# An attention and MLP kernel on one Trainium2 core: part of the splitting of the activations moves from VectorE to GpSimd, GpSimd's work is counted per step, and an order written out by hand begins at unit 2 instead of unit 8

## The chip, the cores and the metric

The kernel runs on one core of one Trainium2 chip. A core has five engines, each with its own instruction queue that is worked off in order: TensorE (PE in the profile, with PEld for its weight loads), VectorE (DVE), ScalarE (ACT), GpSimd (POOL) and SyncE (SP, which here issues every transfer). They meet only in semaphores. The metric is the device time of one execution in microseconds (us).

## The reference

Attention with a learned bias on the distance of positions, for 4 batches, 8 heads, 576 positions and 64 numbers a head, and behind it an MLP with a squared ReLU on the joined heads:

```python
scores = scale * np.matmul(q, k.transpose(0, 1, 3, 2))
x = (psi_rel / psi_i)[..., None]
bias = np.maximum(x @ w1 + b1, 0.0) @ w2
scores = scores + bias.transpose(2, 0, 1)[None, :, :, :]
attn = np.exp(scores - np.max(scores, axis=-1, keepdims=True))
attn = attn / (np.sum(attn, axis=-1, keepdims=True) + 1e-09)
attn_out = np.matmul(attn, v)
...
h = x @ w_in                # x: 2304 x 512, w_in: 512 x 2048
r = np.maximum(h, 0.0)
return (r * r) @ w_out      # w_out: 2048 x 512
```

## The kernel before

**Units.** Attention is cut into 80 units (b, hp, ic): a batch, a pair of heads and a block of 128 queries (ic 0 to 3) or the last 64 (ic 4, the tail, both heads side by side). Units 0 to 39 are batches 0 and 1: first the eight tails (units 0 to 7), then block by block. Units 40 to 79 are batches 2 and 3, five units for each pair of heads, so that units 44, 49, 54, ... 79 are tails. A unit goes through these steps: score products on TensorE (`score_products`, L425) into the one PSUM buffer `sp`; VectorE adds the bias and finds the row minimum (`reduce`, L438, one instruction for each head, only one for a tail), which frees `sp` for the next unit's products; ScalarE takes the exponential (L445); for a tail GpSimd copies 64 columns of the result (L447); TensorE transposes it in two pieces, `pp` (L529) and `pa` (L521), a tail's `pa` reading the copy; ScalarE copies these to `pt` (L851, L1122); TensorE multiplies by v into `px` (L547). When a head pair is done, VectorE inverts its sums (L459, L460), GpSimd makes three low-precision parts of them (L464 to L469), TensorE spreads these (`rp`, `ra`), and VectorE multiplies (L496).

**The bias** is made in the first units: VectorE compares a mask (`bias_mask`, L373), TensorE sums over 32 hidden numbers (`bb`, L383), ScalarE and VectorE scale the two halves (L388, L391) and GpSimd adds them (L399). `mask_upto` and `bias_upto` say how far masks and sums have gone; in the first eight steps each unit but the first two also carries a piece of the remaining mask thresholds (L328 to L332).

**Order.** `step(s)` emits the work of unit s with that of units s - 2 (transposes) and s - 3 (values). For the first `AB * HP` = 8 steps a scheduler orders the instructions of the engines; from step 8 on `manual_schedule` keeps the order in which the code emits them. From unit 40 on the code keeps a list of jobs, each a row of stages (engine, cost in us, function). `fill` takes a stage when its time has come and `room` of its engine is not used up. `room` is refilled at every step for DVE (1.65, or 2.5 at a tail) and ACT; POOL has no entry, so its stages are always taken at once.

**Splitting the activations.** The MLP's first matrix product is done by Strassen's seven products, in two 16-bit parts for each operand. For batch n, `x_scaled` queues products m = 3, 1, 7, 4, 6, 2, 5. Products 2 and 5 take a block of the activations, the other five a sum or difference of two blocks:

```python
stages.append(("POOL", 1.3, lambda m=m: sums_x(0, (m,))))      # L779: the sum, 128 x 512
stages.append(("ACT", 0.71, lambda m=m: high_x(0, (m,))))      # L785: high part, scaled by xsig
stages.append(("DVE", 0.74, lambda m=m: low_x(0, (m,))))       # L792: sum * xsig - high part
```

Batches 0 and 1 are split in this way between units 50 and 79; batches 2, 3 and the tails later, inside the MLP (`split_at`), by the same three functions. Other jobs of the same stretch prepare weights: `lead` (L195 on ACT, L197 to L201 on DVE), `sums_in` (L720 to L722) and the first `high_in` (L734) on POOL, `high_in` (L732) on ACT, `low_in` (L738) on DVE, `rest_out` (L707) on POOL.

**The MLP** begins when attention ends: `products` (`ha`, `hb`, L1191), `sums` (L1205 to L1210), `squares`, `parts_g` and `down` (`y`, L1283).

Of the kernel before, what the change touches and what calls it, by code (L numbers as in the profile page):

```python
# [17 lines left out]
ALU = mybir.AluOpType  # L18
# [4 lines left out]
HP = H // 2  # L23
# [4 lines left out]
AB = 2  # L28
# [49 lines left out]
def attention_then_relu2_mlp(ctx: ExitStack, tc: tile.TileContext, q, k, v, cols, w_in, w_out, psi, xmat, dist, out):  # L78
    nc = tc.nc
    PE, DVE, ACT, POOL, SP = nc.tensor, nc.vector, nc.scalar, nc.gpsimd, nc.sync  # L80
# [64 lines left out]
    NA = len(units)  # L145
# [352 lines left out]
    def scale_x(b, hp, rows_t):  # L498
        times_rows(b, hp, *spread_rows(rows_t))
# [163 lines left out]
    wdst, xsig, alpha_t = {}, {}, {}  # L663
# [72 lines left out]
    def low_in(n, which=(0, 1)):  # L736
# [5 lines left out]
    width = [256] * B + [128]  # L742
    RIGHT = {
        2: ((0, 0), None, None), 5: ((1, 1), None, None), 3: ((0, 1), ALU.subtract, (1, 1)), 4: ((1, 0), ALU.subtract, (0, 0)),
        1: ((0, 0), ALU.add, (1, 1)), 6: ((0, 0), ALU.add, (0, 1)), 7: ((1, 0), ALU.add, (1, 1)),
    }
    ORDER = (2, 3, 4, 5, 1, 6, 7)
    xs_t = {}
# [15 lines left out]
    split_to = [{m: operand(t[:, 512 * (m - 1):512 * m]) for m in range(1, 8)} for t in xs_at]  # L764
# [7 lines left out]
    def sum_of(n, m):  # L772
        return sum_at.get((n, m), sum_at.get(m))

    def sums_x(n, ms):
        for m in ms:
            for cs, op, a, b in halves(n, m):
                if op:
                    POOL.tensor_tensor(out=sum_of(n, m)[:, :, cs], in0=a, in1=b, op=op)  # L779

    def high_x(n, ms):
        for m in ms:
            hi = split_to[n % 2][m][0]
            for cs, op, a, b in halves(n, m):
                ACT.activation(out=hi[:, :, cs], in_=sum_of(n, m)[:, :, cs] if op else a, func=AF.Identity, scale=xsig[n])  # L785

    def low_x(n, ms):
        w = width[n]
        for m in ms:
            hi, lo = split_to[n % 2][m]  # L790
            for cs, op, a, b in halves(n, m):
                DVE.scalar_tensor_tensor(out=lo[:, :, cs], in0=sum_of(n, m)[:, :, cs] if op else a, scalar=xsig[n], in1=hi[:, :, cs], op0=ALU.mult, op1=ALU.subtract)  # L792
            xs_t[n, m] = (hi[:, :, :w], lo[:, :, :w])

    def store_x(n):
        xs_dram[n] = dram.tile([128, 7 * 512], F32, name=f"xs{n}")
        SP.dma_start(out=xs_dram[n], in_=xs_at[n % 2])
# [40 lines left out]
    def step(s, plain=True):  # L838
        loads(s)
        if plain:  # L840
            scores(s)
        else:
            negm, sps = score_products(s, False)
            exps = [reduce(s, n, negm, sp) for n, sp in enumerate(sps)]
        if s and rest:
            tc.keep_in_program_order(rest.pop(0)())
        n, r = divmod(s, AB * HP)

        def turned():
            for dst, src in transposes((s - TL,)):  # L850
                ACT.copy(dst, src)  # L851

        if not plain:
            rows_made(s - TL)
            turned()
            inverted(s - 1)
            if s >= AB * HP * TAIL:
                scan_first(s)
        if n < TAIL:
            if r == 7 and n + 2 < NIC:  # L860
                tc.keep_in_program_order(scale_xc(chunks[n + 2]))
            if plain:
                bias_upto(NJB * n + BO[r])
                if s == AB * HP - 1:
                    mask_upto(done + MB)
            else:

                def then():
                    mask_upto(done + MB + 1)
                    if exps:  # L870
                        exps.pop(0)()

                sum_upto(NJB * n + BO[r], then)
            if r == 1 and n + 2 < NIC:
                load_xc(chunks[n + 2])
        if plain:
            if s >= TL:
                turned()
        else:
            for fn in exps:  # L880
                fn()
        u = s - TL - 1
        if u >= 0:
            for piece in values((u,)):
                keep_values(*piece)
            if u in norm_of:
                b, hp, ic = units[u]
                scale_x(b, hp, norm_of.pop(u))
# [11 lines left out]
        if u in norm_of:  # L900
            norm_of[u] = norm_copy(norm_rows(norm_of[u]))

    for s in range(AB * HP):
        step(s)
    with tc.manual_schedule(engines={PE.engine, DVE.engine, ACT.engine}):
        for s in range(AB * HP, NA):
            step(s, False)

    scan_stack.close()
# [10 lines left out]
    room = {}  # L920
# [95 lines left out]
    def x_scaled(n, ps_col):  # L1016
        scale_of(n, ps_col)
        if n == 0:
            place_x = raw_tile("w2")
            free = [place_x[:, 512 * k:512 * k + 512] for k in range(2)]  # L1020
            for k, ms in enumerate(((3, 1, 7), (4, 6), (2, 5))):
                stages = []
                for m in ms:
                    if RIGHT[m][1]:
                        sum_at[m] = free[k].rearrange("p (c t) -> p c t", c=2)
                        stages.append(("POOL", 1.3, lambda m=m: sums_x(0, (m,))))
                    stages.append(("ACT", 0.71, lambda m=m: high_x(0, (m,))))
                    stages.append(("DVE", 0.74, lambda m=m: low_x(0, (m,))))
                jobs.insert(len(norms), [max(now[0], first[groups[AB * HP + AB]] + 1), stages])
        else:  # L1030
            free = [a.rearrange("p (c t) -> p c t", c=2) for a in (take(1, 4480, 512), take(0, 9856, 512))]
            for k, ms in enumerate(((3, 1, 7), (4, 6), (2, 5))):
                stages = []
                for m in ms:
                    if RIGHT[m][1]:
                        sum_at[n, m] = free[k]
                        stages.append(("POOL", 1.3, lambda m=m: sums_x(n, (m,))))
                    stages.append(("ACT", 0.71, lambda m=m: high_x(n, (m,))))
                    stages.append(("DVE", 0.74, lambda m=m: low_x(n, (m,))))
                job(dest_at[-1] + 1, *stages)  # L1040

    dest_at = [50] + [60] * 6 + [70]
# [49 lines left out]
    sum_at = {}  # L1092
    with tc.manual_schedule():
        job(NA + 1, *(("DVE", 0.68, lambda k=k: scan(k)) for k in range(SCANS, NF)))
        x_job(NA + 4, 0)
        x_job(NA + 7, 1)
        for u in range(NA - TL - 1, NA):
            norm_job(u)
        for s in range(NA, NU + TL + 3):
            now[0] = s  # L1100
            full = s < NU and units[s][2] < TAIL
            room["DVE"] = min(room.get("DVE", 0), 0.3) + (1.65 if full else 2.5)
            room["ACT"] = min(room.get("ACT", 0) + (0.55 if full else 1.9), 0.6 if full else 1.5)
            loads(s)
            if s == NA:
                for tag, name in zip("dbac", ("pa", "pp", "pp", "px")):
                    held[tag] = bank(name, tag)
                for m, tag in enumerate(raws[:NF - SCANS]):
                    fetch_in(ins[SCANS + m], tag)
            if s < NU:  # L1110
                negm, sps = score_products(s, False)
            fill(s, 3)
            px_now[0] = None
            us = [u for u in ((s - 3, s - 2) if s % 2 else (s - 2, s - 1)) if u < NU]
            pieces = []
            sms = [lambda n=n: softmax(s, n, negm, sps[n]) for n in range(len(sps))] if s < NU else []
            if s % 2 == 0:
                if s == NA and NA - 3 in pt_t:
                    for piece in values((NA - 3,), "c"):
                        keep_values(*piece)  # L1120
                for m, c in enumerate(transposes(us, iter("bacb" if s == NA else "abca")) if us else ()):
                    ACT.copy(*c)  # L1122
            else:
                pieces = values(us, "d") if us else []
            fill(s, 0)
            for fn in sms:
                fn()
            if s < NU and ends(s):
                norm_job(s)
            kept = 0  # L1130
            if any(j[0] <= s and j[1][0][0] == "LAST" for j in jobs):
                kept = max(room["DVE"] - 0.6, 0)
                room["DVE"] -= kept
            fill(s, 1)
            fill(s, 2)
            for piece in pieces:
                keep_values(*piece)
            if kept:
                room["DVE"] += kept
                fill(s, 1)  # L1140
# [31 lines left out]
    sum_at = {3: xT[0][:, 0:2, 128:384], 4: xT[0][:, 2:4, 128:384], 1: take(0, 9856, 512).rearrange("p (c t) -> p c t", c=2)}  # L1172
# [121 lines left out]
    with tc.manual_schedule():  # L1294
# [3 lines left out]
        for i in range(NI + 1):  # L1298
# [4 lines left out]
            n, P = items[min(i, NI - 1)]  # L1303
# [102 lines left out]
```

## Time and profile before

| what | us |
|---|---|
| median of 3 runs (714.94 to 715.3) | 715.07 |
| time of the profiled execution | 715.1 |
| its span, first to last instruction | 713.3 |
| PE busy | 685.8 (96%) |
| DVE busy | 552.0 (77%) |
| ACT busy | 474.6 (67%) |
| POOL busy | 196.3 (28%) |

The span is what the trace covers; the remaining 1.8 us lie around it. A timeline row gives start, duration, engine, line and operation, the tile written and read, and in brackets the idle time of the engine ahead of it with what ended it. Rows of one line are merged when they follow one another (x2, x3). A busy PE is one with matmuls under way. A row of waits gives the sum, the number and the longest.

### The profile page before, as it was taken

Reading aid. Unit: us, or ns where it says so; the run is one execution under the profiler, and the core shown is the slowest. Engines: PE = TensorE matmul, PEld = TensorE weight load, DVE = VectorE, ACT = ScalarE, POOL = GpSimd, SP = SyncE. Lnnn points to the kernel's source line nnn. Section 1 sums busy time; section 2 is a strip of 40 time slices with the busy share of each in tenths; the row PEclk is TensorE's granted clock in tenths of the full one; section 3 lists DMA queues with packets and bytes.
Section 4 is the critical chain, followed back from the end, with each engine's and each line's share of the span. In section 5 each row is a group of like instructions: output and inputs, shape, how many; then the busy total and the mean of one; then the engine's idle time right before and its main releaser. Section 6 shows DMA issues by size and latency. Waiting matters only on the chain.

```text
span 713.3 us, 17398 instructions
## 1 busy us (share of the span) xinstructions
PE 685.8 (96%) x6966; PEld 566.9 (79%) x6966; DVE 552.0 (77%) x1165; ACT 474.6 (67%) x954; POOL 196.3 (28%) x313
## 2 busy tenths in 40 slices
PE   7899999999999999999999999999999999999992
PEld 6568888887787877778788888888888888888881
DVE  8998888876788998998888868687567974566761
ACT  5678878878777999997666757765575554464220
POOL 6564544442111344653223113121111220000000
PEclk9999999999999999999999999999999999999996
DMA  6740000007476134101901433230076403433100
GB/s 190 195 131 3 19 2 3 2 12 230 168 243 208 55 88 131 67 31 51 364 1 61 174 137 119 78 144 1 1 251 250 148 19 145 174 107 119 60 2 29
DMA packets 31620, 75.13 MB, mean 105 GB/s; under 512 B 5556, under 2 KB 13876, under 8 KB 30516
## 3 DMA queue, kind: packets, MB, share of 16 engines
q1 hardware_dynamic: 31540, 74.03, 30.8%
q8 instruction: 55, 0.90, 0.5%
q14 instruction: 25, 0.20, 0.1%
HBM read 55.66 MB, written 18.35 MB: 104 GB/s over the span
## 4 chain that ended last, share of the span: by engine, by line
PE 84%; DVE 8%; ACT 3%; issue 2%; POOL 1%; DMA 0%; SPq 0%; ACTq 0%; DVEq 0%; POOLq 0%
PE y L1283 28%; PE ha L1191 13%; PE px L547 10%; PE sp L425 10%; PE hb L1191 9%; PE pp L529 8%; PE bb L383 4%; DVE t L438 2%; DVE mask L373 2%; ACT pt L1122 1%; PE pa L521 1%; DVE bt L391 1%; ACT p L445 1%; DVE xT L496 0%; PE ra L490 0%
## 5 line engine op out<-in xcount | busy, mean ns | idle before, releaser
L1191 PEld LDWEIGHTS <-area 128*128 128x128 f16 x1680 | 147.7, 98 | 25.3 <-issue 8.7
L1283 PE MATMUL y<-w,gh 128*128 128x512 f32 x576 | 149.0, 398 | 0.6 <-ACT gh L1227 0.6
L1283 PEld LDWEIGHTS y<-w,gh 128*128 128x128 f32 x576 | 105.1, 188 | 22.3 <-ACT gh L1227 1.3
L438 DVE CUSTOM_DVE_ANT_0 t<-sp,area 128x576 f32<-128x576 f32 x144 | 104.2, 754 | 23.0 <-PE sp L425 12.4
L445 ACT ACTIVATE p<-t,negm 128x576 f32<-128x576 f32 x144 | 113.3, 798 | 2.6 <-DVE negm L438 2.0
L425 PE MATMUL sp<-k,q 64*128 64x288 f32 (+1 forms) x640 | 98.8, 426 | 3.3 <-DVE negm L438 1.7
L547 PE MATMUL px<-pt,v 128*64 128x128 f32 (+1 forms) x1600 | 92.2, 266 | 0.9 <-DVE bt L391 0.7
L547 PEld LDWEIGHTS px<-pt,v 128*64 128x64 f32 x1600 | 79.2, 137 | 13.5 <-ACT pt L1122 6.4
L1191 PE MATMUL ha<-area 128*128 128x256 f16 (+1 forms) x816 | 85.1, 260 | 0.7 <-DVE c L1208 0.7
L399 POOL TENSOR_TENSOR area<-bt,bt 128x256 f32<-128x256 f32 x72 | 64.8, 907 | 66.1 <-DVE bt L391 65.9
L1283 PE MATMUL y<-w,gl 128*128 128x512 f32 x288 | 79.0, 390 | 0.0
L529 PE MATMUL pp<-ident,p 128*128 128x128 f32 x576 | 77.6, 277 | 0.9 <-DVE bt L391 0.8
L529 PEld LDWEIGHTS pp<-ident,p 128*128 128x128 f32 x576 | 62.4, 141 | 15.5 <-ACT p L445 6.6
L425 PEld LDWEIGHTS sp<-k,q 64*128 64x128 f32 (+1 forms) x640 | 52.8, 175 | 23.5 <-issue 6.5
L1191 PE MATMUL hb<-area 128*128 128x256 f16 (+1 forms) x612 | 64.7, 260 | 0.0
L1283 PEld LDWEIGHTS y<-w,gl 128*128 128x128 f32 x288 | 54.1, 188 | 12.2 <-DVE gl L1228 0.2
L373 DVE TENSOR_TENSOR mask<-sdist,theta 128x1024 f16<-128x1024 f16 x81 | 58.1, 727 | 2.8 <-PE bb L383 0.6
L851 ACT COPY pt<-pp 128x512 f32<-128x512 f32 x68 | 36.9, 589 | 25.4 <-PE pp L529 25.4
L383 PE MATMUL bb<-wmov,mask 128*128 128x64 f16 x1296 | 46.7, 195 | 5.0 <-DVE mask L373 4.8
L383 PEld LDWEIGHTS <-mask 128*128 128x128 f16 x1296 | 43.8, 100 | 9.3 <-DVE mask L373 7.4
L1122 ACT COPY pt<-pp 128x512 f32<-128x512 f32 x76 | 41.5, 605 | 13.3 <-PE pp L529 13.0
L1228 DVE TENSOR_TENSOR gl<-area,gh 128x512 fp32r<-128x512 f32 (+1 forms) x40 | 25.3, 668 | 27.4 <-ACT gh L1227 25.6
(161 smaller groups left out, 993.0 us busy)
## 6 DMA issues: line engine op xcount, KB each, us to landing
raw<-in_w_in SPq DMA_DIRECT2D x32, 512.0 KB, 3.9
r<-in_w_out SPq DMA_DIRECT2D x16, 512.0 KB, 5.1
xs<-area SPq DMA_DIRECT2D x4, 1792.0 KB, 12.7
py<-o SPq DMA_DIRECT2D x12, 512.0 KB, 3.0
o<-py SPq DMA_DIRECT2D x12, 512.0 KB, 4.5
v<-in_v SPq DMA_DIRECT2D x16, 320.0 KB, 4.1
q<-in_q SPq DMA_DIRECT2D x32, 128.0 KB, 3.3
out<-o SPq DMA_DIRECT2D x8, 512.0 KB, 2.9
```

The source lines that it names most:

```text
L373: DVE.tensor_tensor(out=out, in0=win, in1=th, op=ALU.is_ge)
L383: PE.matmul(bb[:, 64 * (7 - r):64 * (8 - r)], lhsT=m[:, r], rhs=wmov[:, n], start=(n == 0), stop=(n == 1))
L399: POOL.tensor_tensor(out=dst, in0=tw, in1=sw, op=ALU.add)
L425: mm = PE.matmul(out_t[to, x, :HALF], lhsT=qt[rows, cols], rhs=kt[rows, k0:k0 + HALF], start=True, stop=True)
L438: DVE.tensor_tensor_reduce(out=t.rearrange("p (x n) -> p x n", x=2), in0=sp[:, :, :HALF], in1=bias.rearrange("p (x n) -> p x n", x=2), sca ...
L445: ACT.activation(out=p[:, S * n:S * n + S], in_=t, func=AF.Exp, bias=negm[:, n:n + 1], scale=-1.0, accum_out=sums[:, 2 * ic + n:2 * ic + n ...
L529: PE.transpose(pp[:, 128 * c:128 * c + 128], p[:, k0:k0 + 128], ident)
L547: PE.matmul(px[64 * h:64 * h + 64, 128 * m:128 * m + w], lhsT=vt[:, c, h], rhs=src, start=(c == 0), stop=(c == 4))
L851: ACT.copy(dst, src)
L1122: ACT.copy(*c)
L1191: PE.matmul(h[:, s, :w], lhsT=a, rhs=x, start=(k == 0), stop=(k == 5))
L1283: PE.matmul(y_t[n][k], lhsT=(gl if m == 2 else gh)[:, slot, o:o + 128], rhs=wl if m == 1 else wh, start=((n, P) in firsts and f == 0 and m ...
```

## The change

For the five products that take a sum, GpSimd now also multiplies the sum by the scale in place (`scaled_sum`), ScalarE only copies it to the 16-bit high part (`high_sum`), and GpSimd, not VectorE, subtracts the high part (`low_sum`). Products 2 and 5 are left as they were. POOL gets 3.2 us of `room` at every step. And the order written out begins at step `FREE` = 2, with the masks made ahead at that step.

```diff
+    def scaled_sum(n, m):
+        sums_x(n, (m,))
+        t = sum_of(n, m)[:, :, :width[n]]
+        POOL.tensor_scalar(out=t, in0=t, scalar1=xsig[n], scalar2=None, op0=ALU.mult)
+
+    def high_sum(n, m):
+        w = width[n]
+        ACT.copy(split_to[n % 2][m][0][:, :, :w], sum_of(n, m)[:, :, :w])
+
+    def low_sum(n, m):
+        w = width[n]
+        hi, lo = (x[:, :, :w] for x in split_to[n % 2][m])
+        POOL.tensor_tensor(out=lo, in0=sum_of(n, m)[:, :, :w], in1=hi, op=ALU.subtract)
+        xs_t[n, m] = (hi, lo)
+
+    def split_stages(n, m, free):
+        if not RIGHT[m][1]:
+            return [("ACT", 0.71, lambda: high_x(n, (m,))), ("DVE", 0.74, lambda: low_x(n, (m,)))]
+        sum_at[n, m] = free
+        return [("POOL", 2.5, lambda: scaled_sum(n, m)), ("ACT", 0.62, lambda: high_sum(n, m)), ("POOL", 1.3, lambda: low_sum(n, m))]
...
-                if s == AB * HP - 1:
+                if s == FREE - 1:
                     mask_upto(done + MB)
...
-    for s in range(AB * HP):
+    FREE = 2
+    for s in range(FREE):
         step(s)
     with tc.manual_schedule(engines={PE.engine, DVE.engine, ACT.engine}):
-        for s in range(AB * HP, NA):
+        for s in range(FREE, NA):
             step(s, False)
...
                 for m in ms:
-                    if RIGHT[m][1]:
-                        sum_at[n, m] = free[k]
-                        stages.append(("POOL", 1.3, lambda m=m: sums_x(n, (m,))))
-                    stages.append(("ACT", 0.71, lambda m=m: high_x(n, (m,))))
-                    stages.append(("DVE", 0.74, lambda m=m: low_x(n, (m,))))
+                    stages += split_stages(n, m, free[k] if k < 2 else None)
                 job(dest_at[-1] + 1, *stages)
...
             room["DVE"] = min(room.get("DVE", 0), 0.3) + (1.65 if full else 2.5)
+            room["POOL"] = min(room.get("POOL", 0), 0) + 3.2
```

What moves, at three places. The first is TensorE around the products of unit 8 (`sp` of 128 rows), before:

```order
L529 MATMUL pp<-ident,p 128x128 x4
L521 MATMUL pa<-ident,p 128x128
L425 MATMUL sp<-k_99,q_102 128x288 x4
L547 MATMUL px<-pt,v 64x64 x10
L529 MATMUL pp<-ident,p 128x128 x4
L521 MATMUL pa<-ident,p 128x128
```

and now:

```order
L383 MATMUL bb<-wmov,mask 128x64
L547 MATMUL px<-pt,v 64x64 x10
L425 MATMUL sp<-k_99,q_102 128x288 x4
L529 MATMUL pp<-ident,p 128x128 x4
L521 MATMUL pa<-ident,p 128x128
L383 LDWEIGHTS mask
```

Before, the values of unit 4 stand behind the products of unit 8; now the values of units 0 to 4 all stand ahead of them, with the same transposes and the same 20 bias sums.

The second place is VectorE behind the two reductions of unit 55 (wa is the scratch tile of a weight's lead, raw holds the sum), before:

```order
L459 TENSOR_SCALAR sums<-sums 128x9
L460 RECIPROCAL sums<-sums 128x9
L792 SCALAR_TENSOR_TENSOR area<-raw,small,area 128x512
L560 COPY xT_3936<-px 128x256
L438 ISA t,negm<-sp,area 128x576
```

and now:

```order
L459 TENSOR_SCALAR sums<-sums 128x9
L460 RECIPROCAL sums<-sums 128x9
L197 TENSOR_SCALAR wa<-wa 128x512
L198 TENSOR_SCALAR wa<-wa 128x512
L197 TENSOR_SCALAR wa<-wa 128x512
L198 TENSOR_SCALAR wa<-wa 128x512
L560 COPY xT_3936<-px 128x256
L438 ISA t,negm<-sp,area 128x576
```

The low part (L792) is gone, and two leads of weights that stood one and three units further back have come in its place.

The third place is GpSimd around the copy for the tail unit 54 (L447; p is the exponential), before:

```order
L779 TENSOR_TENSOR raw<-xT_82 128x512 x2
L447 COPY p<-p 128x64
L779 TENSOR_TENSOR raw<-xT_82 128x512
L720 TENSOR_TENSOR raw<-wa 128x256
L721 TENSOR_TENSOR raw<-wa 128x256
L722 TENSOR_TENSOR raw<-wa 128x128
L734 TENSOR_SCALAR area<-wa,small 128x256
L464 MEMSET parts 128x101
```

and now:

```order
L798 TENSOR_SCALAR raw<-raw,small 128x512
L447 COPY p<-p 128x64
L807 TENSOR_TENSOR area<-raw,area 128x512
L779 TENSOR_TENSOR raw<-xT_82 128x512
L798 TENSOR_SCALAR raw<-raw,small 128x512
L464 MEMSET parts 128x101
```

Each sum is now followed by its scaling (L798), and the low part (L807) comes behind the high part that ScalarE makes; the weight's sums (L720 to L722) stand behind the next low part and sum.

## Rows read from the trace of the kernel before

**Rows 1.** Busy time by stretch: start:end, length, PE, PEld, DVE, ACT, POOL, clock, DMA.

```profile
30.00:40.00 10.00, 8.14 (x146) 5.81 (x144) 9.53 (x21) 5.62 (x15) 6.87 (x10) 1.00 0.68 184
40.00:50.00 10.00, 9.55 (x162) 6.59 (x162) 9.86 (x22) 7.20 (x20) 5.97 (x9) 1.00 0.51 145
240.00:260.00 20.00, 19.49 (x222) 15.38 (x224) 19.40 (x48) 18.80 (x46) 10.74 (x17) 1.00 0.21 58
300.00:320.00 20.00, 19.18 (x231) 15.26 (x227) 18.65 (x39) 18.86 (x47) 11.39 (x16) 1.00 0.08 27
```

**Rows 2.** Waits of PE from 26 to 54 us.

```profile
PE pp L529 <- DVE bt L391: 0.8, 1, 0.8
PE px L547 <- DVE bt L391: 0.7, 1, 0.7
```

**Rows 3.** Waits of PE from 200 to 343 us.

```profile
PE sp L425 <- DVE negm L438: 1.7, 6, 0.4
PE sp L425 <- DVE sums L459: 1.2, 2, 0.6
PE ha L1191 <- DVE c L1208: 0.7, 1, 0.7
PE y L1283 <- ACT gh L1227: 0.6, 1, 0.6
```

**Rows 4.** Timeline of PE, products of unit 8 and values of unit 4.

```profile
52.29 1.24 PE L425 MATMUL sp<-k,q 64*128 64x288 f32 x8
53.50 0.80 PE L547 MATMUL px<-pt,v 128*64 128x64 f32 x20
```

**Rows 5.** Timeline of DVE, masks of the first 54 us.

```profile
14.29 0.88 DVE L373 TENSOR_TENSOR mask<-sdist,theta 128x1024 f16<-128x1024 f16 x1
...
40.15 1.28 DVE L373 TENSOR_TENSOR mask<-sdist,theta 128x1024 f16<-128x1024 f16 x2
```

**Rows 6.** Groups by line and shape: count, busy us, mean ns, idle before.

```profile
L792 DVE SCALAR_TENSOR_TENSOR area<-raw,small,area 128x512 f16<-128x512 f32 x5 | 4.1, 818 | 0.0
...
L707 POOL TENSOR_TENSOR w<-wa,w 128x512 fp32r<-128x512 f32 x16 | 20.6, 1290 | 81.1 <-ACT w L701 81.1
...
L734 POOL TENSOR_SCALAR area<-wa,small 128x256 f16<-128x256 f32 x8 | 7.9, 988 | 0.0
...
L576 POOL CAST ident_b<-ident 128x128 bf16<-128x128 f32 x1 | 0.3, 288 | 0.0
```

**Rows 7.** Timeline of POOL, two sums of batch 1.

```profile
299.63 2.69 POOL L779 TENSOR_TENSOR area<-xT 128x512 f32<-128x512 f32 x2
```

**Rows 8.** Timeline of DVE, a weight's lead beside these sums and one alone.

```profile
250.64 0.43 DVE L198 TENSOR_SCALAR wa<-wa 128x512 int32<-128x512 int32 x1
...
300.23 0.97 DVE L197 TENSOR_SCALAR wa<-wa 128x512 f32<-128x512 f32 x1
301.23 1.38 DVE L198 TENSOR_SCALAR wa<-wa 128x512 int32<-128x512 int32 x1
```

**Rows 9.** Timeline of POOL, the scaling of a weight's first high part.

```profile
269.93 1.17 POOL L734 TENSOR_SCALAR area<-wa,small 128x256 f16<-128x256 f32 x1
```

**Rows 10.** Timeline of DVE, an instruction that starts during it.

```profile
270.27 0.58 DVE L198 TENSOR_SCALAR wa<-wa 128x512 int32<-128x512 int32 x1
```

**Rows 11.** Timeline of DVE, unit 55 and the first reduction of unit 56.

```profile
246.25 0.37 DVE L459 TENSOR_SCALAR sums<-sums 128x9 f32<-128x9 f32 x1
...
248.16 0.76 DVE L438 CUSTOM_DVE_ANT_0 t<-sp,area 128x576 f32<-128x576 f32 x1
```

**Rows 12.** Timeline of PE, products of unit 57, and transposes that read unit 59's copy.

```profile
249.76 1.24 PE L425 MATMUL sp<-k,q 64*128 64x288 f32 x8
...
262.88 0.38 PE L521 MATMUL pa<-ident,p 128*128 128x128 f32 x2
```

**Rows 13.** Timeline of ACT, the high part of the fifth sum of batch 0.

```profile
260.61 0.71 ACT L785 ACTIVATE area<-raw,small 128x512 f16<-128x512 f32 x1
```

**Rows 14.** Timeline of POOL, the sum right behind the copy for unit 54.

```profile
245.30 1.28 POOL L779 TENSOR_TENSOR raw<-xT 128x512 f32<-128x512 f32 x1
```

More of the change, by code (lines that the diff above doesn't have):

```diff
@@ L1023, in x_scaled @@
                 for m in ms:
-                    if RIGHT[m][1]:
[L1025 to L1028, printed above, removed]
+                    stages += split_stages(0, m, free[k].rearrange("p (c t) -> p c t", c=2) if k < 2 else None)
                 jobs.insert(len(norms), [max(now[0], first[groups[AB * HP + AB]] + 1), stages])
@@ L1034, in x_scaled @@
                 for m in ms:
-                    if RIGHT[m][1]:
-                        sum_at[n, m] = free[k]
-                        stages.append(("POOL", 1.3, lambda m=m: sums_x(n, (m,))))
-                    stages.append(("ACT", 0.71, lambda m=m: high_x(n, (m,))))
-                    stages.append(("DVE", 0.74, lambda m=m: low_x(n, (m,))))
+                    stages += split_stages(n, m, free[k] if k < 2 else None)
                 job(dest_at[-1] + 1, *stages)
```

## The prediction

> **What bounds the kernel now.** I read the busy time by stretch first. It says where TensorE has idle time to give back: in 30 to 50 us it stands still for 1.86 + 0.45 = 2.3 us while VectorE is busy for 9.5 and 9.9 of 10 us, and between 240 and 320 us some 0.5 to 0.8 us in 20, with VectorE and ScalarE both busy for 93 to 97% [rows 1]. Nearly everywhere else TensorE is never idle, so a microsecond can be won or lost in these stretches alone, and one won in the first is carried to the end. The waits of TensorE name what ends its idle time. At the start it is VectorE's scaling of the bias halves, which frees the PSUM banks [rows 2]. Between 200 and 343 us it is VectorE's reductions, which free `sp` (1.7 + 1.2 = 2.9 us in eight waits), and at the seam to the MLP two single waits of 0.7 and 0.6 us [rows 3]. So the change can win at most 2.3 + 2.9 + 1.3 = 6.5 us. What it can lose has no such bound.
>
> The sum goes against the profiled execution's own 715.1 us, which is the median of the runs (715.07) to within 0.03. A measurement of this kernel can tell about 0.2%, 1.4 us, from no change.
>
> **The order from unit 2.** VectorE's work ahead of the reductions of unit 8 is the same list in both orders (23 masks and 20 scalings of the query blocks, 8 reductions, five threshold steps); only its mixing differs. As VectorE is the busy engine there, the products of unit 8 can't come much earlier than their 52.3 us [rows 4]. What does move is TensorE's own order: the values of unit 4, 0.80 us, stand behind those products before and ahead of them now, that is, they fill one of the waits. From there on TensorE is the bound, and what it has already done it needn't do later. I take -0.9: 0.8 for this and 0.1 for a slightly earlier product. The best end is all of the idle time, -2.3 [rows 1]. The other end: masks and scalings now alternate strictly. Where they did so at the start, each mask took 0.88 us beside GpSimd's additions; two in a row took 1.28, 0.64 each [rows 5]. Were all 15 masks of units 2 to 7 to cost 0.12 more on average (half of that difference), VectorE would be 1.8 us later and the term +0.9. I take the first because every unit's reduction and threshold step give GpSimd about 1.4 us to finish its additions before the next mask.
>
> **Ten low parts leave VectorE.** Five for each of two batches, 0.818 us each where the sum lies in the raw tile [rows 6]: 8.2 us of VectorE. ScalarE saves 0.71 - 0.62 by the costs in the diff, 0.9 us in all, between waits. Neither is on the path by itself: it can only shorten the 2.9 us of waits above.
>
> GpSimd gets ten scalings and ten subtractions. A subtraction is like the 128x512 one of L707, 1.29 us [rows 6]. A scaling of 128x512 isn't in the trace. The ends are 0.6 us (a cast of 128x128 takes 0.29, at that rate for the part above it) and 2.0 us (twice the 128x256 scaling of L734, 0.99) [rows 6]. I take 1.7, nearest to L734, which is the same operation with the same kind of scalar: its 0.99 less a fixed part of at most 0.29, doubled, plus 0.29. So 10 x (1.3 + 1.7) = 30 us go to an engine that was busy for 10.7 to 11.4 of 20 us there [rows 1].
>
> **What GpSimd does to VectorE.** This decides the second half. While two of GpSimd's sums ran [rows 7], VectorE's L197 took 0.97 us and L198 1.38 us; alone L198 takes 0.43 [rows 8]. They waited about 0.55 and 0.95 us until a sum was over. Beside a scaling the same L198 took 0.58, only 0.15 more [rows 9, 10]. A reduction (one operand in PSUM) takes its 0.76 beside GpSimd's work too [rows 11]. So each sum or subtraction of GpSimd can hold an instruction of VectorE that takes both operands, or its one operand, from SBUF, and there will be ten more of these, and ten scalings.
>
> The Trainium skill, "SBUF — State Buffer", section "Who interferes with whom", says that the pair of ports which VectorE shares with GpSimd is locked for a whole instruction, against VectorE instructions with two SBUF inputs or in a two-port mode. The sums of rows 7 and 8 agree, the scaling of rows 9 and 10 only in part. By that rule taken whole the time would be that of the second rival.
>
> I price it at the one place where it falls on work that has no slack. In unit 55 VectorE went from the norm (L459, at 246.25) to the reductions of unit 56 at 248.16 [rows 11], and TensorE took the products of unit 57 at 249.76, 0.2 us after `sp` came free [rows 12]. Now two leads (four instructions, pairs of 0.8) stand there in place of one low part of 0.75. Without any hold that is 0.3 + 1.6 + 0.35 = 2.25 us from about 245.9 (a low part less ahead), so 248.2, as before. GpSimd, from 245.3 on [rows 14], now goes without a gap through a subtraction (1.3), a sum (1.3) and a scaling (1.7). L459 waits 0.65 for the first, the first L197 about 0.95 for the second, the other three 0.15 each beside the third: 2.05. The reductions start at 250.2 and take 1.4, and TensorE waits until 251.6 instead of 249.76: **+1.9**. One or two of the small waits that follow (1.7 us in six, 0.3 each [rows 3]) go in return, -0.4. That is +1.5. Elsewhere I put the eight low parts that are gone against the holds, at nothing: what covers it is VectorE's step, which with the low part gone has 0.7 to 0.8 us to spare; without that cover each hold costs TensorE its own length.
>
> **GpSimd as a supplier.** Its queue from 245.3 to the copy for unit 59 now holds four subtractions, three sums, three scalings, three weight sums and a first high part: 5.2 + 3.9 + 5.1 + 1.9 + 1.0, and 1.4 of norms, 18.5 us, to 263.8. ScalarE wants the fifth scaled sum at 260.61 [rows 13], and TensorE the copy at about 262.9 [rows 12]. With TensorE 1.5 us later by then, the copy is in time and ScalarE waits about 1.7, mostly in an idle time that it had. I put this at 0; without the delay at unit 55 it would cost 0.5 to 1. The transfers that SyncE issues keep their places but for one weight ahead of a head pair's k and q, which are fetched ten units early.
>
> **The seam.** Behind the last reduction VectorE now has one weight's lead left where it had three, and one weight's low part more. The waits of 0.7 and 0.6 [rows 3] lose their cause; I take -1.0 of 1.3.
>
> **Sum:** 715.1 - 0.9 + 1.5 - 1.0 = **714.7 us**. Its own range is 713.7 to 716.4.
>
> **Rivals.**
> *The relief is real.* VectorE finds gaps between GpSimd's instructions, the scaling costs nearer 0.6, the waits for `sp` fall by a third. For it: the short hold beside the scaling [rows 9, 10]. Against it: the long ones beside the sums [rows 7, 8], and no gap in GpSimd's queue. -1.2 at the start, -0.8 in the middle, -1.2 at the seam: 711.9. Chance 0.34.
> *The holds win.* Besides unit 55 they strike units 61 and 75, where leads of weights now share a step with norms and GpSimd's new work: unit 75 has 3.6 us for VectorE in a step of 3.5 before any hold, and two holds make +1.5; unit 61, with a whole lead beside weight sums of 0.7, +0.6. It decides once GpSimd's queue has no gap longer than one of VectorE's instructions. With 1.5 at unit 55, -0.5 at the seam and -0.3 at the start: 717.9. Chance 0.21.
> *The start goes the other way,* masks held as in rows 5: +0.9 in place of -0.9, 716.5. Chance 0.07.
> That the instructions might not move is excluded by the order itself.
>
> **How the numbers follow.** The forecast has 0.38. Faster by over 0.2% (below 713.6): the first rival and a sliver of the forecast, 0.36. Slower (above 716.5): the second rival and half of the third, 0.24. Between: 0.40. The range runs from the first rival to just below the second, 711.9 to 717.6, which leaves out some 0.1 at either end.
>
> **What would show it.** Right: no TensorE wait on VectorE for unit 8 and values of unit 4 ahead of it; L197 or L198 of over 0.9 us in unit 55 and a wait of over 1 us before the products of unit 57; no wait of 0.7 at `ha`. Wrong: a scaling of under 1 us and no wait in unit 55 (first rival); waits for `sp` of over 5 us in all after 240 us (second); masks of 0.8 us and idle time of over 2.3 us from 30 to 50 us (third).

## The result and the profile after

The changed kernel takes **722.22 us** (median of 5 runs, 720.95 to 722.65) against 715.07 (5 runs of the kernel before beside it): ratio 1.0099, 95% interval 1.0088 to 1.011. The forecast was 714.7 with a range to 717.6, so it is slower by 7.15 us where 0.4 us of gain was expected. The profiled execution took 722.46 us, its span is 720.7 (713.3 before).

The busy time by stretch says where. This view of the kernel after has the columns of [rows 1]:

```profile
30.00:40.00 10.00, 10.00 (x183) 7.78 (x179) 8.82 (x20) 6.46 (x18) 6.22 (x10) 0.92 0.66 185
40.00:50.00 10.00, 9.82 (x181) 7.43 (x178) 10.00 (x22) 6.54 (x20) 6.96 (x9) 1.00 0.48 146
240.00:260.00 20.00, 18.04 (x205) 14.21 (x203) 19.08 (x42) 17.15 (x43) 15.17 (x19) 1.00 0.17 48
260.00:280.00 20.00, 17.50 (x191) 13.77 (x188) 14.73 (x33) 14.34 (x35) 15.23 (x23) 0.91 0.35 100
300.00:320.00 20.00, 17.57 (x205) 14.32 (x205) 19.32 (x38) 17.05 (x43) 17.53 (x21) 1.00 0.09 28
```

From 30 to 50 us TensorE is busy for 2.1 us more than in [rows 1]. From 240 us on it loses 1.4 to 1.9 us in each of the three stretches ([rows 1]; 19.39 before from 260 to 280 us); GpSimd is busy for 15 to 17.5 of 20 us. In the fourth row VectorE *and* ScalarE are under 15 of 20: there TensorE waits for an engine that is not among its usual ones, and its own granted clock is 0.91 of 2.4 GHz on average.

The waits of TensorE from 200 to 343 us, which answer to [rows 3]:

```profile
PE sp L425 <- DVE negm L438: 5.4, 8, 1.3
PE pa L521 <- DVE xT L560: 1.5, 2, 1.0
PE pa L521 <- POOL p L447: 1.2, 1, 1.2
PE sp L425 <- PE px L490: 0.8, 1, 0.8
PE px L547 <- ACT pt L1137: 0.8, 1, 0.8
PE sp L425 <- DVE sums L459: 0.4, 1, 0.4
```

The two waits at the seam (`ha`, `y`) are gone. The waits for `sp` have grown from 2.9 to 5.8 us, and there are new ones: for `pa`, for a copy of GpSimd's, for `pt`.

Where the time goes is seen best from the starts of the score products: for each unit, the start of its products in the kernel after less that in the kernel before (both from the timeline of PE). Less than zero is early.

| place | delay at its end, us | part | the prediction's term |
|---|---|---|---|
| start, units 0 to 9 | -0.91 | -0.9 | -0.9 |
| unit 55 (unit 57's products late) | +1.15 | +2.1 | +1.9 |
| units 57 to 60, waits given back | +0.58 | -0.6 | -0.4 |
| units 60 to 63 | +4.57 | **+4.0** | 0 ("GpSimd as a supplier") |
| units 63 to 79 | +8.86 | **+4.3** | 0 ("Elsewhere ... at nothing") |
| seam to the MLP, to the end of the span | +7.4 | -1.5 | -1.0 |

So three terms came out near what was worked out (the first partly by luck, see below), and the two that were set to nothing hold 8.3 us.

**Unit 55.** VectorE's timeline behind the reductions of unit 55, of the kernel after:

```profile
245.09 0.48 DVE L459 TENSOR_SCALAR sums<-sums 128x9 f32<-128x9 f32 x1
...
245.74 1.44 DVE L197 TENSOR_SCALAR wa<-wa 128x512 f32<-128x512 f32 x1
247.21 0.80 DVE L198 TENSOR_SCALAR wa<-wa 128x512 int32<-128x512 int32 x1
247.93 0.41 DVE L197 TENSOR_SCALAR wa<-wa 128x512 f32<-128x512 f32 x1
248.38 0.71 DVE L198 TENSOR_SCALAR wa<-wa 128x512 int32<-128x512 int32 x1
```

and GpSimd's beside it:

```profile
245.62 1.27 POOL L779 TENSOR_TENSOR raw<-xT 128x512 f32<-128x512 f32 x1
246.99 1.82 POOL L798 TENSOR_SCALAR raw<-raw,small 128x512 f32<-128x512 f32 x1
```

The first lead is held until the sum is over (1.44 us), the others lose up to 0.4 each beside the scaling. The reductions of unit 56 start at 249.34 and TensorE takes unit 57's products at 250.91. This is the wait that the prediction described.

**Units 60 to 63.** GpSimd works without a gap from 244.2 to 273 us. Its timeline at the fifth scaled sum of batch 0, of the kernel after:

```profile
261.16 1.34 POOL L779 TENSOR_TENSOR raw<-xT 128x512 f32<-128x512 f32 x1
262.61 2.05 POOL L798 TENSOR_SCALAR raw<-raw,small 128x512 f32<-128x512 f32 x1
264.61 0.23 POOL L447 COPY p<-p 128x64 f32<-128x64 f32 x1
```

ScalarE's, and then TensorE's, at the same place:

```profile
264.69 0.62 ACT L802 CAST area<-raw 128x512 f16<-128x512 f32 x1 [3.47 <-POOL raw L798]
265.22 1.55 ACT L1137 COPY pt<-pp 128x512 f32<-128x512 f32 x3
```

```profile
264.90 0.33 PE L521 MATMUL pa<-ident,p 128*128 128x128 f32 x1 [1.17 <-POOL p L447]
...
267.16 3.47 PE L547 MATMUL px<-pt,v 128*64 128x128 f32 x40 [0.76 <-ACT pt L1137]
```

ScalarE stands for 3.47 us at the high part, and behind it in its queue stand the copies to `pt` that TensorE needs, which waits 0.76 us for them. The copy for unit 59 comes 1.17 us late, too. In this execution the granted clock, after these idle times of TensorE, is at its lower level from 267.2 to 270.6 us (0.50, which is 1.2 GHz), and those 40 matmuls take 3.47 us instead of the 1.89 that they take at 2.4 GHz in e7_batch0 below: 1.6 more. With one wait of 0.5 for VectorE's reductions that is 1.2 + 0.8 + 1.6 + 0.5, about the 4.0 of the table.

**Units 63 to 79.** VectorE is held at one place after the other. Two of its instructions, then the sums of GpSimd beside them, of the kernel after:

```profile
306.18 1.90 DVE L738 SCALAR_TENSOR_TENSOR area<-raw,small,area 128x640 f16<-128x640 f32 x1
...
309.62 1.69 DVE L792 SCALAR_TENSOR_TENSOR area<-xT,small,area 128x512 f16<-128x512 f32 x1
```

```profile
305.92 1.47 POOL L779 TENSOR_TENSOR area<-xT 128x512 f32<-128x512 f32 x1
...
309.49 1.27 POOL L779 TENSOR_TENSOR area<-xT 128x512 f32<-128x512 f32 x1
```

The groups of VectorE by line and shape from 200 to 345 us, kernel after (columns as in [rows 6]):

```profile
L738 DVE SCALAR_TENSOR_TENSOR area<-raw,small,area 128x640 f16<-128x640 f32 x8 | 8.0, 1005 | 0.0
L201 DVE SCALAR_TENSOR_TENSOR wa<-raw,wa 128x512 uint32<-128x512 uint32 x8 | 7.8, 980 | 0.3
...
L197 DVE TENSOR_SCALAR wa<-wa 128x512 f32<-128x512 f32 x10 | 7.1, 709 | 2.2 <-ACT wa L195 2.2
...
L792 DVE SCALAR_TENSOR_TENSOR area<-xT,small,area 128x512 f16<-128x512 f32 x4 | 5.4, 1347 | 0.0
```

In the kernel before the means of the same four are 878, 830, 507 and 747 ns. With L198, L200 and the smaller L738 the difference, over the instructions of the kernel after, is 1.0 + 1.2 + 2.0 + 2.4 + 0.8 + 0.4 + 0.6 = 8.4 us. The ten low parts that left VectorE had taken 4.3 + 4.1 = 8.4 us there. (The norm's L459 gives back 0.4.) VectorE has won nothing; its time has only moved from its own work into being held: over the whole span it is busy for 552.0 us in both kernels. And where a step was relieved, TensorE gained nothing. In unit 62 VectorE had a whole lead before and has no such job now; it stands idle there, and the delay stays at 4.6 us:

```profile
276.12 0.76 DVE L438 CUSTOM_DVE_ANT_0 t<-sp,area 128x576 f32<-128x576 f32 x1 [1.45 <-PE sp L425]
```

### The profile page after: what moved, and what is told of

The parts are those of the page before. It is cut to its first block, busy times and chain, and to the rows that moved or that the text cites. A ratio compares the mean times of both kernels' runs of the same rounds, so it can differ in the third digit from the quotient of the medians.

```text
span 720.7 us, 17414 instructions
## 1 busy us (share of the span) xinstructions
PE 687.1 (95%) x6966; PEld 568.3 (79%) x6966; DVE 552.0 (77%) x1155; ACT 472.3 (66%) x954; POOL 224.0 (31%) x333
## 4 chain that ended last, share of the span: by engine, by line
PE 82%; DVE 6%; SPq 3%; POOL 3%; ACT 2%; issue 1%; DMA 0%; ACTq 0%; DVEq 0%; POOLq 0%
PE y L1298 28%; PE ha L1206 13%; PE sp L425 10%; PE hb L1206 10%; PE px L547 9%; PE pp L529 7%; PE bb L383 4%; DVE t L438 2%; ACT pt L1137 1%; SPq L169 1%; PE pa L521 1%; SPq L170 1%; POOL raw L798 1%; POOL area L807 1%; POOL raw L779 1%
## 5 line engine op out<-in xcount | busy, mean ns | idle before, releaser
L438 DVE CUSTOM_DVE_ANT_0 t<-sp,area 128x576 f32<-128x576 f32 x144 | 104.1, 753 | 28.3 <-PE sp L425 14.5
L547 PE MATMUL px<-pt,v 128*64 128x128 f32 (+1 forms) x1600 | 93.8, 269 | 0.8 <-ACT pt L1137 0.8
L547 PEld LDWEIGHTS px<-pt,v 128*64 128x64 f32 x1600 | 80.7, 139 | 12.3 <-ACT pt L1137 6.8
L383 PE MATMUL bb<-wmov,mask 128*128 128x64 f16 x1296 | 45.1, 193 | 5.2 <-DVE mask L373 5.0
L707 POOL TENSOR_TENSOR w<-wa,w 128x512 fp32r<-128x512 f32 x16 | 20.6, 1289 | 84.9 <-ACT w L701 84.9
```

Source lines behind the costliest of these rows:

```text
L383: PE.matmul(bb[:, 64 * (7 - r):64 * (8 - r)], lhsT=m[:, r], rhs=wmov[:, n], start=(n == 0), stop=(n == 1))
L438: DVE.tensor_tensor_reduce(out=t.rearrange("p (x n) -> p x n", x=2), in0=sp[:, :, :HALF], in1=bias.rearrange("p (x n) -> p x n", x=2), sca ...
L547: PE.matmul(px[64 * h:64 * h + 64, 128 * m:128 * m + w], lhsT=vt[:, c, h], rhs=src, start=(c == 0), stop=(c == 4))
```

## The experiments

Theory A after the comparison: the start gains, unit 55 loses by a hold, units 60 to 63 by a GpSimd that is late, units 68 to 79 by holds. Its rivals are named in the expectations. For each kernel, the delay of `sp` against the kernel before at five units and at the end of the span, in us, from the timelines of PE and the spans:

| kernel | 54 | 60 | 63 | 70 | 79 | end |
|---|---|---|---|---|---|---|
| the change | -0.9 | 0.6 | 4.6 | 4.9 | 8.9 | 7.4 |
| e1_start | -1.7 | -1.7 | -1.7 | -1.7 | -1.7 | -1.8 |
| e2_split | -0.1 | 1.4 | 5.4 | 5.7 | 9.7 | 8.2 |
| e7_batch0 | -1.7 | -0.2 | 3.7 | 4.0 | 5.3 | 3.5 |
| e8_batch1 | -1.5 | -0.9 | -0.9 | -0.9 | 0.6 | 1.9 |
| e4_late | -1.6 | -0.1 | 1.1 | 1.1 | 2.6 | 3.9 |
| e4b_both | -1.8 | -1.2 | -1.2 | -1.3 | -0.3 | 1.0 |
| e5_noscale | -1.0 | 0.7 | 2.4 | 2.7 | 4.8 | 3.3 |
| e12_none | -1.5 | -1.1 | -0.1 | 0.2 | 1.8 | 0.4 |
| e6_low_dve | -1.0 | 1.0 | 1.0 | 0.9 | 2.0 | 1.1 |
| e13_b0 | -1.6 | -1.1 | -1.1 | -1.2 | -1.2 | -2.1 |

### The parts of the change one by one

e1_start, the kernel before with the order from unit 2:

```diff
-                if s == AB * HP - 1:
+                if s == FREE - 1:
-    for s in range(AB * HP):
+    FREE = 2
+    for s in range(FREE):
-        for s in range(AB * HP, NA):
+        for s in range(FREE, NA):
```

> The kernel before with the order from unit 2 alone. Theory A (the losses of the change lie with GpSimd's new work in units 55 to 79; the order from unit 2 gains): TensorE is 0.9 us ahead from unit 9 on and stays so, 714.2 us. Rival B (the order from unit 2 costs: TensorE waits 2.2 us for the queries of unit 2 and its clock falls to half around 28 to 32 us): the wait and the lower clock show, and the time is 715.1 or more.

713.41 us (713.03 to 714.81, 11 runs), ratio 0.9986 (0.9977 to 0.9994). The order from unit 2 gains by itself (1.7 us in the profiled execution, where A had 0.9), and nothing later takes it back. B falls.

e2_split, the change without it:

```diff
-    FREE = 2
+    FREE = AB * HP
```

> The change without the order from unit 2. Theory A: 722.2 + 0.9 = 723.1 us, unit 8 at 52.3 us, the delays from unit 55 on as in the change. Rival B: the start was part of the loss, 721 or less.

723.16 us, ratio 1.0116 (1.01 to 1.0131), as A says.

e7_batch0 and e8_batch1, the change for one batch (`> 0` and `== 0` in the added line):

```diff
+        if n > 0:
+            return [("POOL", 1.3, lambda: sums_x(n, (m,))), ("ACT", 0.71, lambda: high_x(n, (m,))), ("DVE", 0.74, lambda: low_x(n, (m,)))]
```

> The change for batch 0 alone; batch 1 is split as before. Theory A: -0.9 at the start, +1.5 at unit 55, +4.0 between units 60 and 63 (ScalarE late for the fifth scaled sum, the tail's copy late, TensorE's clock down), nothing after: 715.1 - 0.9 + 1.5 + 4.0 = 719.7 us. Rival C (VectorE's jobs are in a worse order because the planner takes them earlier, wherever GpSimd works): the second half loses over 2 us too, 721.5 or more.

> The change for batch 1 alone; batch 0 is split as before. Theory A: -0.9 at the start, nothing at units 55 to 63, +4.3 in units 68 to 79 by VectorE's instructions held beside GpSimd's, -1.4 at the seam: 715.1 - 0.9 + 4.3 - 1.4 = 717.1 us. Rival C: the delays of units 68 to 79 came from jobs that batch 0 pushed back; without it they vanish, 713 to 714.

718.81 us (ratio 1.0056, 1.0042 to 1.007) and 717.7 us (1.0042, 1.0028 to 1.0056). Each batch has most of its losses at its own place: batch 0 loses 4.0 us between units 60 and 63 here too, batch 1 nothing there, and 2.0 us behind unit 76. But batch 0 alone still loses 1.6 us behind unit 63, though GpSimd has nothing new to do there. That much is C's: jobs of VectorE that were dealt anew. A loss of 0.6 us at unit 58 in e8_batch1 is another thing. VectorE's order there is that of the kernel before, but GpSimd's is not: the room that is now counted for it has put a weight's high part behind the next sum, and this sum so falls beside a lead (VectorE, then GpSimd, of e8_batch1):

```profile
249.14 1.54 DVE L198 TENSOR_SCALAR wa<-wa 128x512 int32<-128x512 int32 x1
```

```profile
249.11 1.28 POOL L779 TENSOR_TENSOR raw<-xT 128x512 f32<-128x512 f32 x1
```

Alone that L198 takes 0.43 [rows 8]. In e7_batch0 TensorE's clock stays at 1.00 from 260 to 280 us, and units 60 to 63 lose the same 4.0 us:

```profile
260.00:280.00 20.00, 16.03 (x182) 12.37 (x178) 14.74 (x35) 14.23 (x35) 14.40 (x23) 1.00 0.30 100
```

So the fall of the clock was not needed for those 4.0 us: without it waits for VectorE (0.5, 1.1 and 0.5 us) took the place of the slow matmuls.

### What is late in units 60 to 63

e4_late, ScalarE's copy of a scaled sum of batch 0 two steps behind the scaling (`scaled_at` notes the step of the scaling):

```diff
-        return [..., ("ACT", 0.62, lambda: high_sum(n, m)), ...]
+        return [..., ("ACT", 0.62, lambda: high_sum(n, m), lambda: now[0] >= scaled_at[n, m] + 2 - n), ...]
```

> The change, with ScalarE's copy of batch 0's scaled sums at the earliest two steps behind the scaling instead of one; the copy of the fifth sum so falls behind the three pt copies that it held up. Theory A (units 60 to 63 lose 4.0 us because ScalarE and TensorE wait for a GpSimd that is behind with its queue): the wait of ScalarE of 3.5 us goes, the values of unit 60 wait no more, TensorE's clock stays up, and unit 63 is 2.4 us less late than in the change; the wait for the tail's copy (1.2 us) stays. 719.8 us if the later units stay as they were. Rival D (the loss there is VectorE held beside GpSimd, and TensorE's waits only follow it): unit 63 as late as in the change, 722 us.

e4b_both, this and the tails' copy on ScalarE:

```diff
-                POOL.tensor_copy(out=p[:, S:S + 64], in_=p[:, S - 64:S])
+                if u < NA:
+                    POOL.tensor_copy(out=p[:, S:S + 64], in_=p[:, S - 64:S])
+                else:
+                    ACT.copy(p[:, S:S + 64], p[:, S - 64:S])
```

> The same, and the tails' copy of 64 columns from unit 40 on made by ScalarE instead of GpSimd. Theory A: no wait of TensorE for that copy, none for pt, units 60 to 63 lose at most 0.5 us; 718.2 to 718.8 us. Rival D: 722 us.

719.27 us (ratio 1.0066, 1.0051 to 1.0081) and 716.75 us (1.0028, 1.0017 to 1.0039). Between units 60 and 63 the change loses 4.0 us, e4_late 1.2, e4b_both nothing, and GpSimd still makes every scaling and subtraction. D falls: the 4.0 us were the wait for a late GpSimd, and what followed from it. e4b_both ends 1.5 us below its range: unit 55 costs 1.1 us there instead of 2.1, and the start gives 0.8 more. TensorE's waits in e4b_both from 236 to 345 us:

```profile
PE sp L425 <- DVE negm L438: 3.0, 5, 1.0
PE ha L1211 <- DVE c L1228: 1.4, 1, 1.4
PE sp L425 <- DVE sums L462: 1.0, 2, 0.6
PE y L1303 <- ACT gh L1247: 0.7, 1, 0.7
PE hb L1211 <- DVE c L1230: 0.3, 1, 0.3
```

No wait for `p` or `pt` is left. The seam, however, costs 1.1 us more than in [rows 3] here (and in e8_batch1 and e4_late): each of these kernels deals VectorE's jobs in another way, and this deal leaves more of them to the seam. So the units behind 63 and the seam have to be read together. The change loses 4.3 us and wins 1.5 back; e8_batch1 and e4_late lose only 1.5 up to unit 79, and 1.3 more at the seam. From unit 63 to the end all three lose 2.8. By this e8_batch1's time came out near what A gave (717.7 against 717.1) without its split: A had 4.3 lost and 1.4 won.

### Scalings, subtractions and the order

e5_noscale, without the scalings, and e12_none, which also fills the low parts with zero:

```diff
-        t = sum_of(n, m)[:, :, :width[n]]
-        POOL.tensor_scalar(out=t, in0=t, scalar1=xsig[n], scalar2=None, op0=ALU.mult)
```

```diff
-        POOL.tensor_tensor(out=lo, in0=sum_of(n, m)[:, :, :w], in1=hi, op=ALU.subtract)
+        POOL.memset(lo, 0.0)
```

> The change without the ten scalings on GpSimd (the high and low parts of the ten products are those of the unscaled sums); the order of the other engines as in the change. Theory A: GpSimd's queue is 17 us shorter, nothing is late in units 60 to 63 (-4.0), unit 55 loses 0.6 less, and of the 4.3 us of units 68 to 79 the part that came from holds beside scalings goes, about half: 715.4 us. Rival D (the sums and subtractions hold VectorE, the scalings hardly do): only what is late goes, 718 us.

> The change without the scalings and with a fill by zero in the place of GpSimd's ten subtractions (the low parts of the ten products are zero, the high parts those of the unscaled sums); the order of all engines as in the change. Theory A: what is left is the order with VectorE ten low parts lighter: start -0.9 to -1.7, no loss at unit 55 beyond 0.5, none later, the seam as it comes: 712.9 to 714.2 us. Rival C (the moved order of VectorE's and ScalarE's jobs costs by itself): 717 us or more.

718.38 us (ratio 1.0049, 1.0032 to 1.0065) and 716.05 us (1.0018, 1.0009 to 1.0028). Both expectations of A fail on the same side: e5_noscale is where rival D put it (718), e12_none between A and C. In e12_none GpSimd's new work is 5.2 us of fills, VectorE has ten low parts less to do than in e1_start (it is busy for 544.7 us in all, against 552.0), and yet TensorE goes from 1.5 us ahead at unit 54 to 1.8 late at unit 79: 3.3 us lost. Its waits from 236 to 345 us:

```profile
PE sp L425 <- DVE negm L438: 5.5, 8, 1.3
PE pa L521 <- DVE xT L560: 0.2, 1, 0.2
```

They come from what VectorE finds at each step. In unit 55 it has the norm and the first halves of two leads ahead of the next reductions, and the norm's first instruction is held by a sum; in unit 61 a whole lead stands where half a lead stood. VectorE's timeline of e12_none, and the sum of GpSimd:

```profile
244.48 1.17 DVE L459 TENSOR_SCALAR sums<-sums 128x9 f32<-128x9 f32 x1
...
265.55 0.62 DVE L197 TENSOR_SCALAR wa<-wa 128x512 f32<-128x512 f32 x1
266.20 0.58 DVE L198 TENSOR_SCALAR wa<-wa 128x512 int32<-128x512 int32 x1
266.81 0.69 DVE L200 SCALAR_TENSOR_TENSOR wa<-raw,wa 128x512 int32<-128x512 int32 x1
267.54 0.85 DVE L201 SCALAR_TENSOR_TENSOR wa<-raw,wa 128x512 uint32<-128x512 uint32 x1
```

```profile
244.21 1.28 POOL L779 TENSOR_TENSOR raw<-xT 128x512 f32<-128x512 f32 x1
```

So theory E: of the 9.8 us between units 54 and 79 the new order (with the old sums) costs 3.3, the subtractions another 2.5 (e5_noscale: 5.8), the scalings 4.0. These are differences between kernels, not prices that hold elsewhere. The order of VectorE is the same in all three. No run takes out the room counted for GpSimd by itself; it is not what moved VectorE's jobs, for written without that line the program gives VectorE the same jobs in the same steps up to unit 74.

e6_low_dve is the counterpart: the scalings alone, with VectorE's order as in e1_start.

```diff
-        POOL.tensor_tensor(out=lo, in0=sum_of(n, m)[:, :, :w], in1=hi, op=ALU.subtract)
+        DVE.tensor_tensor(out=lo, in0=sum_of(n, m)[:, :, :w], in1=hi, op=ALU.subtract)
-        return [..., ("POOL", 1.3, lambda: low_sum(n, m))]
+        return [..., ("DVE", 0.74, lambda: low_sum(n, m))]
```

> The change with the low parts left on VectorE: GpSimd gets the ten scalings alone, and VectorE's order is that of the kernel before with the order from unit 2 (e1_start, 713.4 us). Theory E (three shares: VectorE's jobs dealt anew cost 3.3 us, the subtractions 2.5, the scalings 4.0 because they fill GpSimd's queue on top of the subtractions): with the order unmoved and the queue 13 us shorter the scalings cost 1 to 2 us, 714.4 to 715.4 us. Rival F (the scalings cost their 4 us wherever they stand): 717.4 us.

716.23 us (715.21 to 718.42, 8 runs), ratio 1.0026 (1.0016 to 1.0036); 3.1 us between units 54 and 79. Neither number was met: the scalings cost nearly as much on an unmoved order, so theory E's reason for their share (a queue already filled by the subtractions) was not needed. Half of it (1.6 us between units 58 and 60) is lateness again, at another place. ScalarE, then TensorE, at unit 58 of e6_low_dve:

```profile
255.51 0.62 ACT L802 CAST area<-raw 128x512 f16<-128x512 f32 x1 [2.30 <-POOL raw L798]
```

```profile
256.35 0.66 PE L529 MATMUL pp<-ident,p 128*128 128x128 f32 x4 [1.69 <-ACT rows L479]
```

The rest comes at units 77 and 78, where VectorE's L459 (1.03 us) and L738 (1.60) are held beside sums.

### Is there a relief at all, and a better start

e13_b0 is e4b_both with the line of e7_batch0; e14_free3 and e14_free4 are e1_start with `FREE` = 3 and 4.

> e4b_both for batch 0 alone: what was late there is mended, batch 1 is split as before. Theory E (VectorE's relief is worth nothing, as TensorE waits for VectorE for 2.9 us in all here and those waits lie in steps that got other jobs): units 55 to 63 give back 0.4, 713.8 us, not below e1_start's 713.4. Rival G (the relief is real and was only covered): 712.5 us or less.

> e1_start with the written order from unit 3. In e1_start TensorE stands still for 2.2 us ahead of unit 2 and is ahead of the kernel before by 0.2 us only there; its 1.65 us come between units 5 and 9. Theory E: the wait is filled with bias sums again, and the same 1.7 us are won later; 713.0 to 713.4 us, with a narrower spread since TensorE's clock has no cause to fall there. Rival: units 2 to 4 are what the gain rests on, 714.5 us or more.

> e1_start with the written order from unit 4. Theory E as for unit 3: 713.0 to 713.4 us. Rival: the scheduler's order of units 2 and 3 keeps part of the loss, 714 us or more.

e13_b0: 713.24 us (712.88 to 713.85, 10 runs), ratio 0.9982 (0.9973 to 0.9991), which e1_start's interval covers. It loses 0.5 us up to unit 60 and wins them back at the seam. So five low parts off VectorE, with nothing late, are worth nothing that these runs can tell; G falls. e14_free3 and e14_free4: 713.84 (ratio 0.9992, 0.9984 to 1.0001) and 713.87 us (0.999, 0.9981 to 0.9999), both above the expected 713.0 to 713.4. Their profiled executions end 2.0 and 1.4 us earlier than that of the kernel before, but no median is below e1_start's, and e14_free3's runs spread as widely (713.11 to 715.2), so the expected narrower spread is not there. By their ratios e1_start and e13_b0 are 1.0 and 1.3 us faster than the kernel before, the best of this study.

## Why the prediction was wrong

**What held.** The start: -0.91 at unit 9 against -0.9, with the values moved ahead of unit 8's products as said. That the number was met is partly luck: the values bring 0.64, and unit 8's products come 0.27 earlier in an execution that was at 1.2 GHz for 3.4 us of the start, where 0.1 was put. In e1_start, at full clock, they come 1.0 earlier and the lead is 1.7; most kernels with that order have 1.5 to 1.7, which the bound of -2.3 allowed. Unit 55: +2.1 and -0.6 against +1.9 and -0.4, with the L197 of over 0.9 us and a wait of 0.94 us before the products of unit 57, behind another of 1.02 before the transposes. (The recorded sum itself gives 2.04, from 248.16 to 250.2; its 1.9 forgot the 0.2 us from the free `sp` to the products.) The scaling, at 1.7 us from bounds of 0.6 and 2.0: 1.73 and 1.95 on average. The seam: both waits gone, -1.5 against -1.0. This term hangs on the deal of VectorE's jobs, as the prediction had it: e12_none, on the change's order and little late, gains 1.4 there, e1_start on the old order 0.1. But it is no gain by itself: a deal that leaves less to the seam has put it into the units before (2.8 us lost from unit 63 to the end, with and without the gain at the seam).

**The step that failed first: "GpSimd as a supplier ... I put this at 0".** The list of its queue was right, and so was "TensorE 1.5 us later": the start moved both engines ahead by 0.9, and from there TensorE had lost 1.5 at unit 60. But the queue, from 244.38 to the copy for unit 59 at 264.61, took 20.2 us and not 18.5: scalings 5.4 for 5.1, sums 4.2 for 3.9, and 1.0 more for the weight's sums, its high part and the norms, each a little longer than its row. So the copy, priced with 0.6 us in hand, came 1.17 late, and ScalarE waited 3.47 us instead of 1.7. And "mostly in an idle time that it had" looked at ScalarE alone and not at what is queued behind the waiting instruction: three copies to `pt`, and TensorE behind these. The place cost 4.0, which e4_late and e4b_both took away while GpSimd kept every scaling and subtraction. Even without the delay at unit 55 the text allowed only 0.5 to 1.

**The second: "I put the eight low parts that are gone against the holds, at nothing".** As busy time that came out, 8.4 us against 8.4 for all ten. As a term of the path it was wrong, because relief and holds do not meet at the same place. A step that is relieved gives TensorE nothing where TensorE was the bound anyway (unit 62); a step that is filled or held beyond what it has to spare costs the excess (this is argued from units 55 and 61, and was not measured step by step). The planner refills what the low parts leave with leads of weights (3.3 us of loss in e12_none, with the old sums and the fills still on GpSimd), and the holds then fall on those. This was 4.3 us behind unit 63, 2.8 of them net of the seam.

**The rivals.** *The holds win* named units 61 and 75 and the right condition, its sign came true (5.5 us of waits for `sp` after 240 us, where over 5 was the mark), unit 75's step cost 1.2 us where it had 1.5, and e12_none loses 1.0 at unit 61; but it priced the second half at 3.6 us in all, without the late supply, and ended at 717.9. *The relief is real* had the largest chance of a gain and is contradicted by e13_b0 and e12_none: TensorE waited for VectorE for 2.9 us in the whole stretch, and not in the steps that were relieved. The range missed because it was built from one failure at a time.

**Readings that were off without weight.** [rows 2] leaves out four smaller waits of the same stretch, those for masks (0.9 us) among them, and from 280 to 300 us of the kernel before TensorE is idle for 0.9 us with VectorE at 90%, outside the "0.5 to 0.8" and "93 to 97%".

## What to carry to other kernels

Work that is moved to an idle engine also makes that engine a supplier. Before pricing it, list each thing that others take from its queue and, for each taker, what stands behind the waiting instruction in the taker's own queue; an idle engine that is filled without a gap for 29 us hands every delay on. Moving work off a busy engine wins only at steps where that engine ends the wait; busy time saved against busy time lost says nothing of the path. And where a planner deals out jobs by room, taking a job away deals all the later ones anew: compare the list of each step with what the step has to spare.

## What the runs showed of the hardware

**Holds go by the kind of GpSimd's instruction.** In the change, from 200 to 345 us, each of the nine instructions of VectorE of 1.4 us or more stands beside a sum or a subtraction of GpSimd (two operands in SBUF) and ends after it (L197 beside the sum in unit 55: 1.44 instead of 0.41). Beside the scaling, one operand and a scalar, L198 took 0.71 and 0.80 instead of 0.43. The Trainium skill, "SBUF — State Buffer", section "Who interferes with whom", has the shared pair of ports locked for a whole instruction; for the sums and subtractions the trace agrees, for the scalings it does not: they slow VectorE and let it through.

**The slowing is mutual, and a scaling is dear.** The groups of GpSimd from 200 to 345 us, kernel after:

```profile
L798 POOL TENSOR_SCALAR area<-area,small 128x512 f32<-128x512 f32 x5 | 9.8, 1951 | 0.5
L798 POOL TENSOR_SCALAR raw<-raw,small 128x512 f32<-128x512 f32 x5 | 8.6, 1725 | 1.8 <-DVE small L225 1.4
...
L807 POOL TENSOR_TENSOR area<-raw,area 128x512 f16<-128x512 f32 x5 | 6.3, 1258 | 0.0
...
L807 POOL TENSOR_TENSOR area<-area 128x512 f16<-128x512 f32 x5 | 5.8, 1163 | 0.0
```

Of the ten scalings of 128x512, the four that L738 or L792 of VectorE runs into take 2.03 to 2.40 us, the other six 1.57 to 1.82; that is more than a subtraction of the same size with its two operands (1.16 or 1.17 in nine of ten, 1.65 in the other).

**The clock at the start.** The order from unit 2 makes TensorE stand still for 2.2 us ahead of unit 2. Two stretches, 26 to 30 and 30 to 34 us, of e1_start (columns as in [rows 1]):

```profile
26.00:30.00 4.00, 1.76 (x24) 1.13 (x21) 4.00 (x9) 1.82 (x4) 3.17 (x5) 1.00 0.64 183
30.00:34.00 4.00, 4.00 (x78) 3.28 (x78) 4.00 (x9) 2.86 (x8) 2.57 (x5) 1.00 0.75 228
```

In the change the same two stretches, with the same wait, have a granted clock of 0.78 and 0.79: 2.4 GHz at first, and 1.2 GHz (0.50) from 28.3 to 31.6 us, behind the wait. With the lower clock the lead at unit 9 was mostly 0.9 to 1.0 us, with the full one 1.5 to 1.7. Why the same wait costs the clock in one execution and not in another was not settled, nor why e14_free3, which hasn't that wait, spreads as widely.
